# Regrouping the state, decay and factor work of blocks 0 and 1, and a last store in two row halves

## The chip, the cores and the metric

The kernel runs on one core of a Trainium2 chip. The metric is the device time of one execution in microseconds (us). A core has five engines that run side by side, each through its own instructions in order: TensorE (PE, with its weight loads listed as PEld), VectorE (DVE), ScalarE (ACT), GpSimd (POOL) and SyncE (SP, which here only issues transfers). An instruction that needs another engine's result waits on a semaphore, and everything behind it on its own engine waits with it. PE's results go to PSUM, which this kernel lays out as eight tiles of 128 x 512 float32, called banks here; what POOL takes of PSUM is copied to SBUF by ACT first.

## The reference

A chunked state-space layer (4 batches, 8 heads, 768 positions, head size 32, state size 16) is followed by a bilinear feed-forward layer over 3072 tokens of width 256 and inner width 1536.

```python
# per batch and head, chunk c of 32 positions
cum = np.cumsum(log_a[c]);  L = np.exp(cum[:, None] - cum[None, :]) * causal
y[c] = ((C @ B.T) * L) @ x  +  (C @ state) * np.exp(cum)[:, None]
state = np.exp(cum[-1]) * state + (B * np.exp(cum[-1] - cum)[:, None]).T @ x
# then, with heads and head sizes side by side as 256 columns
out = ((y @ w_a) * (y @ w_b)) @ w_out
```

The chunk length doesn't change the result, and the kernel takes chunks of 128.

## The kernel before

**Tiling.** The 768 positions are six blocks of 128. A block holds two "pairs"; pair p belongs to block p // 2. Block 0 (pairs 0 and 1) is treated batch by batch with its own code; from block 1 on (pairs 2 to 11) the work is laid out by batch in `planes`, turned into `BT` and `CT` by a VectorE transpose (`turn`). The running product of `a` within a block stands in `Pr`, its middle row's inverse in `rmid`, and the decay factors are made from both: `fB`, `fC` (lines 781, 790, 871) for block 0 and the state of block 1, `FC` and its inverse `FB` for the planes, `fCl` and `fBl` for the states of the later blocks.

**Factors.** `mid_rows` (286) multiplies `Pr` by `rmid` into `Ps` on POOL. `turned_rows` (296) is a VectorE transpose of `Ps` into `Pt`; `batch_factors` (301) copies `Pt` into `FC`, one copy for each of four batches, on ACT or on POOL; `batch_inverse` (308) is a VectorE reciprocal into `FB`; `late_factors` (311) and `late_inverse` (315) make `fCl` and `fBl` on VectorE. `scale_q` (341, called twice by `prep`) multiplies B or C by `FB` or `FC` into `planes` on POOL; `scale_bc` (324) does so for the states' B.

**Layer and states.** `scores` (398) is the small matmuls C·B into the four banks `SC`; `mask` (442) multiplies a bank by the causal table, on VectorE, or by an ACT copy and POOL; `pv1` (522) and `outputs` (532) multiply by x and copy the result out as `X2T` (block 0) or `XB`. `ds_mm` (495) makes a block's contribution to the state, and `gps` (852) spreads the blocks' decays over the state's rows; ACT copies it to `G` (861), from which POOL makes `Ge` (880), `spair` (576) and `gV` (586).

**Feed-forward.** A unit is a group of matmuls with `Wa` (`aps`), one with `Wb` (`bps`), an ACT copy of `aps` to SBUF (`evac_a`, 610, tile `asb`) and a VectorE product of `bps` and `asb` into `hk` or `hkb`. For block 0 a unit is (pair, k2) with four matmuls of 256 columns in each group (`unit_mm`, 593; `times`, 615); for later blocks it is `bunit(blk, k)` (659), with two of 512 columns. `out_mm`, `out_store` (634, 646) and `bout` (685) multiply by `Wo` and store.

**Order.** The schedule is manual: each engine runs its instructions in the order of the calls from line 774 on. Half of the PSUM banks are `SC`; the other four hold, one tile each, whatever `bank()` hands out, and the string `BANKS` (22) says which bank the n-th tile gets. A tile's first matmul waits until the tile before it in that bank has been read: an `aps` by its ACT copy, a `bps` by its VectorE product. The first tile (`fps`, factors and `gps`) keeps bank 0 until line 871 has read it; the next tile in that bank is the nineteenth, `aps` of unit (0, 4) (line 888).

**Transfers.** Loads of x as f16 and of the weights are issued by POOL (they change the type), all others by SP or ACT. `load_wo` (187) issues half of `Wo`. `bout(last, 3, 2)` (1036) ends the kernel: two halves of 128 columns, each with its own copy out of PSUM and its own store, the first by SP, the second by ACT (709).

Of the kernel before, what the change touches and what calls it, by code (L numbers as in the profile page):

```python
# [19 lines left out]
SS = 64.0  # L20

BANKS = (
    "012313213212312312031203123021032103120312013201320130231021302130231203120312013023102310"
    "2312013201320132012301230123012301230123012301320132013201320132013201320132013201320"
)


# [1 line left out]
def kernel(  # L29
# [13 lines left out]
    nc = tc.nc  # L43

    nb, H, S, D = x.shape
# [5 lines left out]
    NK = d_ff // 128  # L51
    NQ = NK // 2
    BH = nb * H
    NBP = nb // 2
# [74 lines left out]
    def bank(name):  # L129
        return psf.tile([128, 512], f32, name=name, tag=f"ff{next(banks)}")  # L130
# [56 lines left out]
    def load_wo(half):  # L187
        return nc.gpsimd.dma_start(
            Wo[:, 6 * half : 6 * half + 6].rearrange("p (g kk) e -> p g (kk e)", kk=3),
            moe_w_out.rearrange("(g p kk) e -> p g (kk e)", p=128, kk=3)[:, 2 * half : 2 * half + 2],  # L190
        )
# [94 lines left out]
    def mid_rows(lo, hi, eng):  # L286
        k = slice(lo + NBLK - NT, hi + NBLK - NT)
        eng.tensor_tensor(
            out=Ps[:, lo:hi], in0=Pr[:, k], in1=rmid[:, k].unsqueeze(2).broadcast_to((BH, hi - lo, Q)), op=ALU.mult
        )  # L290
# [5 lines left out]
    def turned_rows(lo, hi):  # L296
        nc.vector.transpose(
            Pt[:, lo:hi].rearrange("p k s c -> p (k s) c"), Ps[:, lo:hi].rearrange("p k (i s) -> p k s i", s=4)
        )
# [8 lines left out]
    def batch_inverse(lo, hi):  # L308
        nc.vector.reciprocal(FB[:, lo:hi], FC[:, lo:hi])

    def late_factors(lo, hi):
        for c0 in range(32 * lo, 32 * hi, 32):
            nc.vector.transpose(fCl[c0 : c0 + 32], Ps[:, NT - NL :, c0 : c0 + 32])
# [4 lines left out]
    def flat(f, lo, hi):  # L318
        return f[:, lo:hi].rearrange("p k r b h -> p (k r b h)")
# [175 lines left out]
    def ds_mm(p, DS):  # L495
        s, bp = st[p], p % NBP
        st["DS", p // NBP] = DS
        DS = DS.rearrange("p (g d) -> p g d", d=2 * D)
        for bt, g in itertools.product(range(2), range(4)) if p >= P2 else ():
            row = 32 * (2 * bp + bt)  # L500
            nc.tensor.matmul(  # L501
                DS[row : row + 32, g],
                s["bm"][:, bt, 2 * g : 2 * g + 2, :].rearrange("p h n -> p (h n)"),
                by_token(s["X16"])[:, bt, 2 * g : 2 * g + 2].rearrange("p h d -> p (h d)"),
                start=True,
                stop=True,
                skip_group_check=True,
                tile_position=(0, row),
            )
        for r, g, bt in itertools.product(range(2), range(4), range(2)) if p < P2 else ():  # L510
            k, row = slice(64 * bt, 64 * bt + 64), 32 * (2 * bp + bt)
            nc.tensor.matmul(
                DS[row : row + 32, g],
                s["bm"][k, r, 2 * g : 2 * g + 2, :].rearrange("p h n -> p (h n)"),
                s["X16"][k, 2 * g : 2 * g + 2, r, :],
                start=(r == 0 and g == 0),
                stop=(r == 1),
                skip_group_check=True,
                tile_position=(64 * bt, row),
            )  # L520

    def pv1():
        PY = [SC1[:, bt, 0:256] for bt in range(2)]
        for u in range(2):
            pv_u(1, u, PY, True)
        o_ = X2T[:, 1].rearrange("p t u q -> p t (u q)")
        i_ = SC1[:, :, 0:256]
        c0 = nc.scalar.activation(out=o_[:, 0], in_=i_[:, 0], func=AF.Copy, scale=YS / SS)
        c1 = nc.vector.tensor_scalar(o_[:, 1], i_[:, 1], YS / SS, None, ALU.mult)
        tc.declare_no_dep(c1.ins, c0.ins.name, reason="reads of two banks")  # L530
# [79 lines left out]
    def evac_a(a_ps, on_dve=False):  # L610
        asb = ffh.tile([128, 512], f32, name="asb", tag="asb")
        (nc.vector.tensor_copy if on_dve else nc.scalar.copy)(asb, a_ps)  # L612
        return asb
# [12 lines left out]
    def unit(p, k2, between=None, by_pool=False):  # L626
        a_ps = unit_mm(p, k2, Wa)
        if between:
            between()
        b_ps = unit_mm(p, k2, Wb)  # L630
        asb = evac_a(a_ps)
        return lambda: times(p, k2, b_ps, asb, by_pool)

    def out_mm(p, bt, o_ps, ks):
        hk = st[p]["hk"]
        for k in ks:
            nc.tensor.matmul(  # L637
                o_ps[:, 0:d_model],
                hk[:, k, bt * Q : (bt + 1) * Q],
                Wo[:, k, :],  # L640
                start=(k == 0),
                stop=(k == NK - 1),
                skip_group_check=True,
            )
# [36 lines left out]
    def bgo(blk, *ks):  # L681
        for k in ks:
            bunit(blk, k)()

    def bout(blk, c, parts=1):
        hk = st[("FF", blk)]["hk"]
        rows = out[c * S + blk * Q :][0:Q]
        w = d_model // parts
        for part in range(parts):
            o_ps = bank("ops")  # L690
            cs = slice(part * w, part * w + w)
            for k in range(NK):
                nc.tensor.matmul(  # L693
                    o_ps[:, 0:w],
                    hk[:, k, c * Q : (c + 1) * Q],
                    Wo[:, k, cs],
                    start=(k == 0),
                    stop=(k == NK - 1),
                    skip_group_check=True,
                )  # L700
            o_sb = outp.tile([128, d_model], f32, name="osb", tag="osb")
            if parts > 1 and part == 0:
                nc.vector.tensor_scalar(o_sb[:, 0:w], o_ps[:, 0:w], 1.0 / (YS * YS), None, ALU.mult)
            else:
                nc.scalar.activation(out=o_sb[:, 0:w], in_=o_ps[:, 0:w], func=AF.Copy, scale=1.0 / (YS * YS))  # L705
            if blk * NBP < P0:
                stores.append(lambda rows=rows, o_sb=o_sb: nc.sync.dma_start(rows, o_sb))
            else:
                (nc.sync, nc.scalar)[part].dma_start(rows[:, cs], o_sb[:, 0:w])

    def loads_b(*ps):
        for p in ps:
# [16 lines left out]
    def loads_x(p):  # L729
        if p < NP:  # L730
            load2(nc.gpsimd, p, 2)

    def go(*items):
        for p, k2 in items:
            unit(p, k2)()
# [111 lines left out]
    loads_b(4, 5)  # L847
    times(0, 0, bps[0], asb[0])
    times(0, 1, bps[1], asb[1], by_pool=True)
    pv1()  # L850
    ds_mm(1, SC[0][:, 0:256])
    gps = fps[:, 96 : 96 + H // 2 * NG]
    nc.tensor.matmul(
        gps,
# [3 lines left out]
        stop=True,  # L858
        skip_group_check=True,
    )  # L860
    nc.scalar.copy(G.rearrange("p g k -> p (g k)"), gps)
    times(0, 2, bps[2], asb[2])
    turned_rows(0, 1)
    load_wo(0)
    batch_factors(0, 1, *range(nb), eng=nc.gpsimd)
    mid_rows(1, NT, nc.gpsimd)
    go((1, 0))
    batch_inverse(0, 1)
    go((1, 1))
    ds_mm(0, SC[0][:, 0:256])  # L870
    nc.vector.reciprocal(flat(fB, 1, 2), fps[:, 2 * NBP * H : 4 * NBP * H])
    go((1, 2))
    scale_q(2, 1, nc.gpsimd)
    scale_q(3, 1, nc.gpsimd)
    scale_q(2, 0, nc.gpsimd)
    load_wo(1)
    scale_q(3, 0, nc.gpsimd)
    state_sums(0)
    late_factors(0, 3)
    nc.gpsimd.tensor_tensor(  # L880
        out=Ge.rearrange("p k (g e) -> p g k e", e=2),
        in0=G.unsqueeze(3).broadcast_to((128, H // 2, NG, 2)),
# [4 lines left out]
    late = ((0, 3), (0, 4), (1, 3))  # L887
    aps = [unit_mm(p, k2, Wa) for p, k2 in late]
    asb = [evac_a(a_ps) for a_ps in aps]
    for (p, k2), a_sb_ in zip(late, asb):  # L890
        times(p, k2, unit_mm(p, k2, Wb), a_sb_)
        if k2 == 4:
            turn(2)
    go((0, 5))
    h = unit(1, 4, lambda: scores(2))
    turn(3)
    mask(product(2, 3), by_pool=True)
    mask(product(2, 0))
# [2 lines left out]
    mask(product(2, 2), by_pool=True)  # L901
    load_q(nc.gpsimd, 2, ALL_Q[6:])
    mask(product(2, 1))
    turned_rows(1, 2)
    o = [bank("ops"), bank("ops")]
    out_mm(0, 0, o[0], range(6))
    out_mm(0, 1, o[1], range(6))
    batch_factors(1, 2, 0, 1)
    h5()
    scores(3)  # L910
    mask(product(3, 3), by_pool=True)
    batch_factors(1, 2, 2, 3)
# [5 lines left out]
    )  # L918
    for m in range(3):
        mask(product(3, m))  # L920
    batch_inverse(1, 2)
    turned_rows(2, NT)
    for bt in range(2):
        o.append(bank("ops"))
        out_mm(1, bt, o[-1], range(6))
    for f in x_in:
        f()
    for c in range(3):
        p, bt = divmod(c, NBP)
        out_mm(p, bt, o[c], range(6, NK))  # L930
        if c == 2:
            batch_factors(2, NT, *range(nb))
        out_store(p, bt, o[c])
    loads_q(3)
    prep(4)
    prep(5)
    loads_x(4)
    late_factors(3, 4)
    late_inverse(0, NL)
    outputs(1)  # L940
    state_sums(1)
    batch_inverse(2, NT)
    prep_b(4, 5)
    loads_b(6, 7)
    out_mm(1, 1, o[3], range(6, NK))
# [8 lines left out]
    for m in range(3):  # L954
        mask(product(4, m))
        if m == 0:
            loads_x(6)
            prep(6)
        if m == 1:
            turn(5)  # L960
        bgo(1, *range(4 + 3 * m, min(7 + 3 * m, NK)))
    scores(5)
    mask(product(5, 3), by_pool=True)
    prep(7)
# [102 lines left out]
```

## Time and profile before

| | |
|---|---|
| time, median of 3 runs (lowest, highest) | 123.44 us (123.11, 123.44) |
| the profiled execution's own time | 122.69 us |
| its span, first to last instruction | 120.8 us |
| granted TensorE clock over the span | 1.000 |
| DMA moved | 12.13 MB, mean 100 GB/s |

| stretch, us | PE | DVE | ACT | POOL busy, us |
|---|---|---|---|---|
| 10 to 15 | 4.83 | 4.55 | 3.62 | 3.23 |
| 15 to 20 | 5.00 | 4.06 | 3.48 | 3.41 |
| 20 to 25 | 5.00 | 4.92 | 2.99 | 4.91 |
| 25 to 30 | 4.96 | 4.93 | 4.02 | 4.92 |
| 40 to 45 | 4.97 | 5.00 | 2.73 | 3.83 |
| 110 to 121 | 7.55 | 1.84 | 2.70 | 0.00 |

The busy time of PE counts each matmul from its start to a modelled end, and a matmul's end overlaps the next one's start, so PE is busy by this count even in a pause of some tenths of a microsecond. Pauses are better read from the starts of successive groups: a group of four matmuls of 256 columns, or of two of 512, takes 0.43 to 0.44 us from its start to the next group's.

### The profile page before, as it was taken

The page shows a single profiled execution, that of the slowest core. Times are in us where ns is not written, and L with a number is a line of the kernel's source. Part 1 is how long each engine was busy: PE and PEld are TensorE (multiplying, and loading weights), DVE is VectorE, ACT ScalarE, POOL GpSimd, SP SyncE. Part 2 cuts the span into 40 slices and gives each one's busy share as a digit, 9 for nine tenths or more (in the row PEclk, how much of TensorE's full clock was granted, in tenths as well). Part 3 has the DMA queues.
Part 4 walks back from the last instruction along what each step waited for, and adds up shares of the span by engine and source line. Part 5 has one row for each costly group of instructions (what it writes and reads, how often), then busy time and mean ns, then how long its engine had stood idle before and what let it go on. Part 6 is the DMA issues. An engine that isn't in the chain of part 4 may idle for free.

```text
span 120.8 us, 3551 instructions
## 1 busy us (share of the span) xinstructions
PE 115.9 (96%) x1385; PEld 73.9 (61%) x1386; DVE 90.2 (75%) x166; ACT 67.9 (56%) x136; POOL 58.8 (49%) x92
## 2 busy tenths in 40 slices
PE   7989999999999999999999999999999999999990
PEld 2436789888644488544485464775465684645880
DVE  5998988999798994599966999686899426758000
ACT  0446756769776646567666646635735637475230
POOL 7994986999699969387803994200000000000000
PEclk9999999999999999999999999999999999999999
DMA  3999999894789994959992929012001111010132
GB/s 63 135 183 192 207 230 197 134 200 113 99 94 161 115 139 101 110 68 121 218 241 89 85 9 121 5 46 87 5 6 40 43 49 44 0 43 0 43 108 71
DMA packets 59297, 12.13 MB, mean 100 GB/s; under 512 B 54480, under 2 KB 59216, under 8 KB 59280
## 3 DMA queue, kind: packets, MB, share of 16 engines
q0 software_dynamic: 20320, 3.80, 38.9%
q1 hardware_dynamic: 36432, 7.74, 34.8%
q10 hardware_dynamic: 2528, 0.36, 1.8%
q8 instruction: 11, 0.18, 0.7%
q14 instruction: 6, 0.05, 0.1%
HBM read 12.42 MB, written 3.15 MB: 129 GB/s over the span
## 4 chain that ended last, share of the span: by engine, by line
PE 92%; DVE 4%; issue 0%; ACT 0%
PE ops L693 22%; PE aps L667 22%; PE bps L667 21%; PE ops L637 5%; PE aps L598 4%; PE SC L404 4%; PE bps L598 3%; DVE t L449 3%; PE SC L238 3%; PE SC L473 2%; PE SC L536 1%; PE tc L238 1%; PE py L458 1%; PE SC L485 1%; DVE bt L385 1%
## 5 line engine op out<-in xcount | busy, mean ns | idle before, releaser
L612 ACT COPY asb<-aps 128x512 f32<-128x512 f32 x72 | 42.0, 587 | 17.2 <-PE aps L667 13.4
L679 DVE TENSOR_TENSOR hkb<-bps,asb 128x512 f16<-128x512 f32 x60 | 40.2, 687 | 12.7 <-ACT asb L612 11.1
L667 PE MATMUL aps<-XB,Wa 128*128 128x512 f16 x120 | 35.7, 379 | 0.0
L667 PE MATMUL bps<-XB,Wb 128*128 128x512 f16 x120 | 35.7, 379 | 0.0
L693 PE MATMUL ops<-Wo,hkb 128*128 128x256 f16 (+1 forms) x252 | 28.1, 268 | 0.0
L693 PEld LDWEIGHTS <-hkb 128*128 128x128 f16 x252 | 23.0, 98 | 3.8
L667 PEld LDWEIGHTS <-Wb 128*128 128x128 f16 x120 | 12.4, 103 | 13.6
L667 PEld LDWEIGHTS <-Wa 128*128 128x128 f16 x120 | 12.1, 103 | 11.7 <-issue 0.5
L449 DVE TENSOR_TENSOR t<-SC,causal_q 128x512 f16<-128x512 f32 x27 | 17.3, 681 | 2.4 <-PE SC L404 2.4
L705 ACT ACTIVATE osb<-ops 128x256 f32<-128x256 f32 (+1 forms) x20 | 7.6, 379 | 18.4 <-PE ops L693 18.4
L447 POOL TENSOR_TENSOR t<-tmp,causal_q 128x512 f16<-128x512 f32 x5 | 5.8, 1161 | 10.0 <-ACT tmp L446 10.0
L177 POOL DMA_DIRECT2D xn<-in_x_dram x8 | 9.5, 1192 | 0.0
L346 POOL TENSOR_TENSOR planes<-cq,FC 128x256 f16<-128x256 f32 x10 | 7.6, 775 | 2.2 <-DMA cq<-in_C_dram 2.1
L622 DVE TENSOR_TENSOR hk<-bps,asb 128x512 f16<-128x512 f32 x11 | 7.2, 672 | 0.9 <-ACT asb L612 0.8
L346 POOL TENSOR_TENSOR planes<-bq,FB 128x256 f16<-128x256 f32 x10 | 7.7, 772 | 0.4 <-DMA bq<-in_B_dram 0.4
L449 DVE TENSOR_TENSOR t<-SC,causal 128x512 f16<-128x512 f32 x11 | 7.0, 675 | 0.4 <-PE SC L404 0.3
L598 PE MATMUL aps<-X2T,Wa 128*128 128x256 f16 x48 | 6.8, 274 | 0.0
L446 ACT COPY tmp<-SC 128x512 f32<-128x512 f32 x10 | 5.9, 589 | 1.5 <-PE SC L404 1.1
L598 PE MATMUL bps<-X2T,Wb 128*128 128x256 f16 x48 | 6.6, 273 | 0.0
L558 ACT ACTIVATE XB<-SC 128x512 f16<-128x512 f32 (+1 forms) x9 | 4.6, 547 | 3.5 <-PE SC L501 2.4
L447 POOL TENSOR_TENSOR t<-tmp,causal 128x512 f16<-128x512 f32 x5 | 5.8, 1161 | 0.0
L637 PE MATMUL ops<-Wo,hk 128*128 128x256 f16 x48 | 5.8, 273 | 0.0
(101 smaller groups left out, 109.2 us busy)
## 6 DMA issues: line engine op xcount, KB each, us to landing
out_dram<-osb SPq DMA_DIRECT2D x23, 128.0 KB, 1.8
cq<-in_C_dram SPq DMA_DIRECT2D x20, 64.0 KB, 3.9
bq<-in_B_dram SPq DMA_DIRECT2D x18, 64.0 KB, 3.8
bn<-in_B_dram SPq DMA_DIRECT2D x8, 128.0 KB, 4.1
xn<-in_x_dram POOLq DMA_DIRECT2D x8, 128.0 KB, 5.9
Wa<-in_moe_w_a_dram POOLq DMA_DIRECT2D x2, 384.0 KB, 7.3
Wb<-in_moe_w_b_dram POOLq DMA_DIRECT2D x2, 384.0 KB, 7.9
Wo<-in_moe_w_out_dram POOLq DMA_DIRECT2D x2, 384.0 KB, 6.5
```

What stands on the lines that cost most here:

```text
L177: eng.dma_start(by_token(pair_in[p][which]).rearrange("p t h n -> p (t h) n"), src.rearrange("t h q n -> q (t h) n"))
L346: eng.tensor_tensor(out=plane[:, c0 : c0 + 4 * step].rearrange("p (j c) s -> p j s c", c=step)[:, :, :, 0:N], in0=by_batch[blk][which][:, ...
L447: nc.gpsimd.tensor_tensor(out=o_, in0=tmp, in1=c_, op=ALU.mult)
L449: nc.vector.tensor_tensor(out=o_, in0=i_, in1=c_, op=ALU.mult)
L598: nc.tensor.matmul(ps[:, kk * 2 * Q : (kk + 1) * 2 * Q], W[k // 6][:, f, k % 6 // 3 * 384 : (k % 6 // 3 + 1) * 384].rearrange("p (c kk) -> ...
L612: (nc.vector.tensor_copy if on_dve else nc.scalar.copy)(asb, a_ps)
L622: eng.tensor_tensor(out=s["hk"][:, 2 * k2 : 2 * k2 + 2, :].rearrange("p k q -> p (k q)"), in0=b_ps, in1=asb, op=ALU.mult)
L637: nc.tensor.matmul(o_ps[:, 0:d_model], hk[:, k, bt * Q : (bt + 1) * Q], Wo[:, k, :], start=(k == 0), stop=(k == NK - 1), skip_group_check= ...
L667: nc.tensor.matmul(t_, W[k // 6][:, f, k % 6 // 3 * 384 : (k % 6 // 3 + 1) * 384].rearrange("p (c kk) -> p kk c", kk=3)[:, k % 3], XB[:, b ...
L679: return lambda: nc.vector.tensor_tensor(out=s["hk"][:, k], in0=ps[1], in1=asb, op=ALU.mult)
L693: nc.tensor.matmul(o_ps[:, 0:w], hk[:, k, c * Q : (c + 1) * Q], Wo[:, k, cs], start=(k == 0), stop=(k == NK - 1), skip_group_check=True,)
L705: nc.scalar.activation(out=o_sb[:, 0:w], in_=o_ps[:, 0:w], func=AF.Copy, scale=1.0 / (YS * YS))
```

## The change

Nothing that is computed changes, and no load. What moves or is regrouped:

- `gps` is made before `pv1`; `ds_mm(0)` follows `ds_mm(1)` at once, and the copy to `G` is VectorE's in place of ACT's; the reciprocal of line 871 follows it, ahead of the product of unit (0, 2).
- `load_wo(1)` is issued four POOL operations earlier.
- `turned_rows` for blocks 2 to 5 is one call in place of two, in the place of `late_factors(0, 3)`, which moves behind the masks of pair 3; `batch_factors(2, NT)` moves ahead to the units at 890; `batch_inverse(1, NT)` is one call in place of two.
- `scores(2)` stands behind both groups of unit (1, 4), not between them.
- `out_mm(1, 0)` stands ahead of `scores(3)`, not behind it.
- `outputs(1)` and `state_sums(1)` stand ahead of `late_factors(3, 4)` and `late_inverse`.
- `turn(5)` stands behind unit 4 of block 1, not behind the mask that precedes unit 7.
- The second half of the last store is issued as rows 0 to 63 by ACT and rows 64 to 127 by SP.
- `BANKS` has another order.

```diff
 BANKS = (
-    "012313213212312312031203123021032103120312013201320130231021302130231203120312013023102310"
-    "2312013201320132012301230123012301230123012301320132013201320132013201320132013201320"
+    "012313213212301230123012302103120312301230132013210320132012301230132103210321023013201320"
+    "1321023102310231021302130213021302130213021302310231023102310231023102310231023102310"
 )
...
+            elif part == 0:
+                nc.sync.dma_start(rows[:, cs], o_sb[:, 0:w])
             else:
-                (nc.sync, nc.scalar)[part].dma_start(rows[:, cs], o_sb[:, 0:w])
+                for eng, h in ((nc.scalar, slice(0, 64)), (nc.sync, slice(64, 128))):
+                    eng.dma_start(rows[h, cs], o_sb[h, 0:w])
...
-    pv1()
-    ds_mm(1, SC[0][:, 0:256])
     gps = fps[:, 96 : 96 + H // 2 * NG]
     nc.tensor.matmul(
         gps,
...
-    nc.scalar.copy(G.rearrange("p g k -> p (g k)"), gps)
+    pv1()
+    ds_mm(1, SC[0][:, 0:256])
+    ds_mm(0, SC[0][:, 0:256])
+    nc.vector.tensor_copy(G.rearrange("p g k -> p (g k)"), gps)
+    nc.vector.reciprocal(flat(fB, 1, 2), fps[:, 2 * NBP * H : 4 * NBP * H])
     times(0, 2, bps[2], asb[2])
     turned_rows(0, 1)
     load_wo(0)
     batch_factors(0, 1, *range(nb), eng=nc.gpsimd)
     mid_rows(1, NT, nc.gpsimd)
+    load_wo(1)
     go((1, 0))
     batch_inverse(0, 1)
     go((1, 1))
-    ds_mm(0, SC[0][:, 0:256])
-    nc.vector.reciprocal(flat(fB, 1, 2), fps[:, 2 * NBP * H : 4 * NBP * H])
     go((1, 2))
     scale_q(2, 1, nc.gpsimd)
     scale_q(3, 1, nc.gpsimd)
     scale_q(2, 0, nc.gpsimd)
-    load_wo(1)
     scale_q(3, 0, nc.gpsimd)
     state_sums(0)
-    late_factors(0, 3)
+    turned_rows(1, NT)
...
     asb = [evac_a(a_ps) for a_ps in aps]
+    batch_factors(2, NT, *range(nb))
     for (p, k2), a_sb_ in zip(late, asb):
         times(p, k2, unit_mm(p, k2, Wb), a_sb_)
         if k2 == 4:
             turn(2)
     go((0, 5))
-    h = unit(1, 4, lambda: scores(2))
+    h = unit(1, 4)
+    scores(2)
     turn(3)
...
     mask(product(2, 1))
-    turned_rows(1, 2)
     o = [bank("ops"), bank("ops")]
     out_mm(0, 0, o[0], range(6))
     out_mm(0, 1, o[1], range(6))
     batch_factors(1, 2, 0, 1)
     h5()
+    o.append(bank("ops"))
+    out_mm(1, 0, o[2], range(6))
     scores(3)
...
-    batch_inverse(1, 2)
-    turned_rows(2, NT)
-    for bt in range(2):
-        o.append(bank("ops"))
-        out_mm(1, bt, o[-1], range(6))
+    batch_inverse(1, NT)
+    late_factors(0, 3)
+    o.append(bank("ops"))
+    out_mm(1, 1, o[3], range(6))
...
-        if c == 2:
-            batch_factors(2, NT, *range(nb))
         out_store(p, bt, o[c])
...
     loads_x(4)
+    outputs(1)
+    state_sums(1)
     late_factors(3, 4)
     late_inverse(0, NL)
-    outputs(1)
-    state_sums(1)
-    batch_inverse(2, NT)
...
-        if m == 1:
+        k0 = 4 + 3 * m
+        bgo(1, k0)
+        if m == 0:
             turn(5)
-        bgo(1, *range(4 + 3 * m, min(7 + 3 * m, NK)))
+        bgo(1, *range(k0 + 1, min(k0 + 3, NK)))
```

## The prediction

> **What bounds the kernel now.** I read the page's engine shares and chain first, then the waits of PE, then the timeline.
>
> ```profile
> PE 115.9 (96%) x1385; PEld 73.9 (61%) x1386; DVE 90.2 (75%) x166; ACT 67.9 (56%) x136; POOL 58.8 (49%) x92
> ...
> PE 92%; DVE 4%; issue 0%; ACT 0%
> ```
>
> PE is the chain: 92% of it, and from 14.85 us to 117.6 us nothing else. The count of matmuls doesn't change, so only pauses between groups, PE time spent on changing between kinds of matmul, and the tail can change. The starts of groups in the timeline (start, length, engine, line) show them:
>
> ```profile
> 12.16 1.55 PE L598 MATMUL bps<-X2T,Wb 128*128 128x256 f16 x12
> ...
> 13.64 0.45 PEld L458 LDWEIGHTS <-xn 64*32 64x32 f16 x32 [0.20 <-issue]
> ...
> 13.86 0.42 PE L458 MATMUL SC<-t,xn 64*32 64x128 f16 x32
> ...
> 14.37 0.42 DVE L529 TENSOR_SCALAR X2T<-SC 128x256 f16<-128x256 f32 x1
> 14.43 0.29 PEld L853 LDWEIGHTS fps<-hsx,indm 32*128 32x128 f32 x2
> ...
> 14.85 0.62 PE L598 MATMUL aps<-X2T,Wa 128*128 128x256 f16 x4
> ...
> 16.20 0.60 PE L598 MATMUL bps<-X2T,Wb 128*128 128x256 f16 x4
> ...
> 16.73 0.41 PE L512 MATMUL SC<-xn,bm 64*32 64x64 f16 x16
> ```
>
> Four places lose time. (a) `pv1` has its weights at 13.64 but starts at 13.86, when VectorE's mask has ended (13.80): 0.22 us. (b) `ds_mm(0)` breaks the units: from bps at 16.20 to the second bps after it at 17.52 are 1.32 us where two periods of 0.4375 are due, so it costs 0.445, of which 0.09 is the change of tile size ahead of it (16.20 to 16.73 is 0.53, not 0.44). (c) and (d) are here:
>
> ```profile
> 23.89 1.47 PE L637 MATMUL ops<-Wo,hk 128*128 128x256 f16 x12
> ...
> 24.67 0.68 DVE L449 TENSOR_TENSOR t<-SC,causal 128x512 f16<-128x512 f32 x1
> ...
> 25.40 0.65 PE L404 MATMUL SC<-turned 32*64 32x128 f16 x32
> ...
> 39.91 1.85 DVE L679 TENSOR_TENSOR hkb<-bps,asb 128x512 f16<-128x512 f32 x3
> 39.98 0.59 PE L667 MATMUL bps<-XB,Wb 128*128 128x512 f16 x2
> ...
> 40.61 0.59 PE L667 MATMUL aps<-XB,Wa 128*128 128x512 f16 x2
> ```
>
> (c) Twelve matmuls at 0.109 and the size change of 0.09 should lead to `scores(3)` at 25.29; it starts at 25.40, behind VectorE's last mask (24.67 + 0.68): 0.11 us. (d) 39.98 to 40.61 is 0.63 where 0.43 is the rule: 0.20 us, because the bank is that of bps 7, whose product is the first of VectorE's three from 39.91.
>
> **The change, part by part.**
>
> *gps, pv1 and both ds_mm.* `gps` now starts in pause (a), at 13.64; its input is ready since 12.62 (POOL, 12.41 + 0.21). The rows bound its price: 0.29 (its two weight loads) to 0.42 (14.43 to 14.85, but that end was set by VectorE's copy, 14.37 + 0.42). I take 0.29, as the next small loads need wait for nothing else: `pv1` at 13.93, 0.07 later than now (0.20 at the other end). Then `pv1` 0.25, `ds_mm(1)` 0.33 and `ds_mm(0)` 0.34 end at 14.85. VectorE's copy of `X2T` starts 0.51 behind `pv1`, at 14.44, ends at 14.86, and aps (1, 0) starts 0.06 behind it, as now, at 14.92. So `ds_mm(0)` lies wholly under that copy: **-0.445 + 0.07**.
>
> *VectorE behind it.* Its instructions overlap by 0.08 when nothing holds them. New ahead of product (0, 2) are the copy to `G` and the reciprocal. No row has the copy on VectorE; copies from PSUM of 128 and 256 columns are 0.29 and 0.42, so 20 columns give some 0.18 (bounds 0.15, its shortest reciprocal, and 0.29). G 14.78 to 14.96, reciprocal (0.34) to 15.22, product (0.68) to 15.82, `turned_rows` (0.39) to 16.13. POOL's four copies to `FC` take 0.96 (15.86 to 16.82 now), so 16.21 to 17.17. The product of (1, 0), which waits for ACT's copy, is done at 16.94; next in VectorE's queue is `batch_inverse`, which stands until 17.20 (now 16.85, when VectorE had just come free) and ends at 17.56. Queued behind it is the product of (1, 1), 17.48 to 18.14. **Who waits: PE.** By the new string aps (0, 4) takes the bank of bps (1, 1), while before it took that of `fps`. PE, in steps of 0.4375 from 14.92, would be there at 18.00 and must wait until 18.20: **+0.20** (0 if `FC` is copied faster or G is short, 0.35 with the long G and late POOL). All other banks of the new order are free in time: bps (1, 1) wants bank 1 at 16.25 (read until 15.82), bps (1, 2) bank 3 at 17.12 (17.00), bps (0, 3) bank 3 at 19.07 (18.80).
>
> *turned_rows(1, NT) and the four ACT copies.* POOL's `mid_rows` (1.04) follows `FC`: ready at 18.29. VectorE reaches the transpose at 18.66. Its price: 128 columns 0.374, 384 columns 0.776, so 512 give 0.98 by the slope, 1.58 as four times 0.394; I take 0.98, since 384 already lie on that slope: done at 19.64, about as `late_factors` now (19.87). ACT's four copies (0.25 to 0.27 each, 1.09 with gaps) then run from 19.92, behind the copy of aps (1, 3), to 21.01. Queued behind is the copy of aps (0, 5), wanted at 21.06; it ends at 21.65, and bps (1, 4) takes that bank at 21.70: **0**, with no cover to spare.
>
> *load_wo(1).* Its 0.76 of issue lies at 18.29 to 19.05 in POOL's idle time (now idle until 19.32, when the C of block 1 has landed): 0; and `scale_q(3, 0)` comes 0.75 earlier. Its data go ahead of x and B of block 1 in the queues: x of pairs 2 and 3 landed at 24.05, ACT's casts want it at 27.4, so 1.9 (384 KB at the 200 GB/s of these slices) can be hidden.
>
> *scores(2) behind unit (1, 4).* Planes still end at 21.31, `turn(2)` at 21.92; PE comes there at 22.14, so 0.
>
> *out_mm(1, 0) ahead of scores(3).* Its 0.66 covers pause (c): VectorE's mask ends at 25.35, PE comes at 25.67 with 0.09 of size change to go: **-0.11**.
>
> *Inverse, late factors, outputs(1).* VectorE ends pair 3's masks at 28.37, `batch_inverse` of 128 columns (0.95, as `fBl`) at 29.24, three transposes of 0.30 at 30.09; its copy to `XB` is wanted at 30.15. Cover 0.06, then 0.13 more before PE needs `XB`: 0.
>
> *turn(5).* Behind product 4 (ends 37.17) it lasts to 37.66, product 5 is 0.23 late, product 6 on time, the mask ends at 39.50, so product 7 ends at 40.07 and not at 40.55; aps 10 wants its bank at 40.41: **-0.20**.
>
> *The last store.* The tail:
>
> ```profile
> 117.59 0.28 ACT L705 ACTIVATE osb<-ops 128x128 f32<-128x128 f32 x1 [0.96 <-PE ops L693]
> 117.90 0.38 ACTq L709 DMA_DIRECT2D out_dram<-osb  x1
> ```
>
> SP ends its own issue at 117.65 and then only waits, so both halves start at 117.90. The issue costs 0.65 for 512 pieces and 0.45 for 256, 0.0008 a piece: 64 rows in place of 128 save 0.05. Landing takes 1.6 for 64 KB and 1.8 to 1.9 for 128 KB, so half the bytes would save 0.15 if each half had engines to itself. Bounds +0.10 (SP's half late) and -0.20; I take **-0.06**. By the Trainium skill (DMA: Bandwidth & Descriptors, Rules for kernel authors) two transfers to disjoint partition halves aren't worth making, as both are spread over the same 16 engines; only issue time is saved. By that rule this term would be -0.05, and the further 0.14 in rival 1 is not to be had; no row here shows two such halves.
>
> **Sum**: -0.445 + 0.07 + 0.20 - 0.11 - 0.20 - 0.06 = **-0.55**. Against the profiled execution (span 120.85, time 122.69; 1.84 lies around the span) that gives 120.3 and 122.14. The median of the runs shown is 0.75 above that execution; on it the forecast is **122.9**. About 0.3% (0.37 us) is what a measurement of this kernel can tell from no change.
>
> **Rivals.**
>
> 1. *No wait at aps (0, 4), store at its best.* For it: the wait of 0.20 hangs on 0.26 that VectorE stands before `batch_inverse`, a chain of four short instructions. Against: each link has a row. -0.55 - 0.20 - 0.14 = -0.89: **122.55**. Chance 0.18.
>
> 2. *The bank takes the gain.* VectorE's delay is at its upper end: G 0.29 and later POOL copies make the wait 0.35; `gps` costs 0.42 (+0.13); the store gives nothing (+0.06). -0.55 + 0.15 + 0.13 + 0.06 = -0.21: **123.2**, the same. For it: bounds of rows; against: all three together. Chance 0.20.
>
> 3. *ACT stands on `Pt` (slower).* Place: the four ACT copies ahead of the copy of aps (0, 5). From `Pt` at 19.64 on, every 0.1 costs PE 0.1 at bps (1, 4). With the transpose at 1.58, `Pt` comes at 20.24, ACT ends at 21.63, aps (0, 5) is copied at 22.24 and bps (1, 4) starts at 22.30, +0.60; from +0.55 on it decides. With the long `gps` as well (+0.13) and the store at +0.10: -0.55 + 0.60 + 0.13 + 0.16 = +0.34: **123.8**. For it: no cover at all there; against: the slope of the two transposes. Chance 0.15.
>
> **How the numbers follow.** Forecast 0.47 (122.65 to 123.1), rivals 0.18, 0.20, 0.15. Predicted 122.9. The range takes in rivals 1 and 2 and the nearer part of 3: 122.3 to 123.6. Faster by over 0.3%: forecast and rival 1, 0.65; within: rival 2 and 0.02 of rival 3, 0.22; slower: 0.13.
>
> **What would show it.** `gps` ahead of `pv1`, `pv1` near 13.93 and aps (1, 0) near 14.92, with no small matmuls up to `scores(2)`; a step of some 0.64 in place of 0.44 before aps (0, 4); no wait before `scores(3)`; even steps of 0.43 through block 1's units; ACT's `FC` copies ended by 21.05 and bps (1, 4) without a step; two half issues at the same time and an end some 2.9 us behind them. It is wrong if a step of over 0.3 appears at aps (0, 4), bps (1, 4) or the first matmul on `XB`.

## The result, and the profile after

The changed kernel is slower: 123.37 us median of 21 runs against 122.86 us of 21 runs of the kernel before, a ratio of 1.0037 with a 95% interval of 1.0025 to 1.0048. One of the changed kernel's 21, at 137.4 us with a granted clock of 0.857, is left out of the ratio. Its profiled execution took 123.15 us with a span of 121.45 us; before these were 122.69 and 120.85.

The page's engine shares and its chain, after:

```profile
PE 115.1 (95%) x1385; PEld 73.4 (60%) x1386; DVE 90.2 (74%) x165; ACT 67.5 (56%) x135; POOL 58.6 (48%) x92
...
q8 instruction: 11, 0.18, 0.6%
...
PE 88%; DMA 4%; SPq 2%; DVE 2%; issue 1%; ACT 0%; DVEq 0%
```

PE's busy time falls by 0.8 us though it runs the same 1385 matmuls: somewhere it now stands, long enough to show in this count. Where, the waits of PE show (line and what it waited for, us in total, times, longest):

```profile
PE SC L238 <- PEq L1055: 0.8, 1, 0.8
PE SC L512 <- issue: 0.7, 1, 0.7
```

The first was there before. The second is new: line 512 is `ds_mm`, its 0.7 us are counted from the modelled end of the matmul before, and "issue" means that no wait which the profile shows explains it. In the timeline after:

```profile
13.75 0.39 PE L854 MATMUL fps<-hsx,indm 32*128 32x20 f32 x2
...
14.07 0.42 PE L458 MATMUL SC<-t,xn 64*32 64x128 f16 x32
...
14.32 0.45 PE L512 MATMUL SC<-xn,bm 64*32 64x64 f16 x25
...
14.59 0.42 DVE L529 TENSOR_SCALAR X2T<-SC 128x256 f16<-128x256 f32 x1
14.94 0.17 DVE L865 COPY G<-fps 128x20 f32<-128x20 f32 x1
...
15.49 0.27 PE L512 MATMUL SC<-xn,bm 64*32 64x64 f16 x7 [0.71 <-issue]
...
15.70 0.62 PE L598 MATMUL aps<-X2T,Wa 128*128 128x256 f16 x4
```

`gps` stands ahead of `pv1`, as planned, and VectorE's copy of `X2T` ends at 15.02, so aps (1, 0) could start at 15.08. But 25 of the 32 matmuls of the two `ds_mm` run, the last of them starts at 14.59 and the next matmul only at 15.49, and aps (1, 0) starts at 15.70: 1.62 us behind `pv1` and not 1.00.

The pauses that the change was forecast to remove are gone. Ahead of `scores(3)`, and in block 1's units:

```profile
24.28 2.13 PE L637 MATMUL ops<-Wo,hk 128*128 128x256 f16 x18
26.34 0.65 PE L404 MATMUL SC<-turned 32*64 32x128 f16 x32
...
40.26 0.59 PE L667 MATMUL bps<-XB,Wb 128*128 128x512 f16 x2
40.69 0.59 PE L667 MATMUL aps<-XB,Wa 128*128 128x512 f16 x2
```

Eighteen matmuls at 0.109 and the size change of 0.09 make the 2.06 from 24.28 to 26.34, and 40.26 to 40.69 is the even step of 0.43.

The end, after:

```profile
117.67 0.28 ACT L705 ACTIVATE osb<-ops 128x128 f32<-128x128 f32 x1 [0.96 <-PE ops L693]
117.97 0.55 SPq L712 DMA_DIRECT2D out_dram<-osb  x1
117.98 0.57 ACTq L712 DMA_DIRECT2D out_dram<-osb  x1
```

Two issues of half the rows last 0.55 and 0.57 where one of all rows lasted 0.38. From the end of the last copy to the end of the span it is 3.50 us; before it was 2.98.

So in the two profiled executions the last copy ends 0.08 later (117.95 against 117.87) and the tail is 0.52 longer: the difference of the spans is 0.60, nearly all of it behind the last matmul. The 0.62 of the new pause has eaten the middle's gain.

### The profile page after: what moved, and what is told of

The parts are those of the page before. It is cut to its first block, busy times and chain, and to the rows that moved or that the text cites. A ratio compares the mean times of both kernels' runs of the same rounds, so it can differ in the third digit from the quotient of the medians.

```text
span 121.5 us, 3551 instructions
## 1 busy us (share of the span) xinstructions
PE 115.1 (95%) x1385; PEld 73.4 (60%) x1386; DVE 90.2 (74%) x165; ACT 67.5 (56%) x135; POOL 58.6 (48%) x92
## 4 chain that ended last, share of the span: by engine, by line
PE 88%; DMA 4%; SPq 2%; DVE 2%; issue 1%; ACT 0%; DVEq 0%
PE ops L693 22%; PE aps L667 22%; PE bps L667 21%; PE aps L598 5%; PE ops L637 4%; PE bps L598 4%; DMA bn<-in_B_dram 4%; PE SC L404 3%; PE SC L473 2%; SPq L153 2%; PE SC L536 1%; PE SC L485 1%; DVE t L449 1%; PE SC L512 0%; DVE cm L333 0%
```

## Experiments

The ratios are to the kernel before, run on the same chip.

**The split store alone.** The kernel before with this edit only:

```diff
+            elif part == 0:
+                nc.sync.dma_start(rows[:, cs], o_sb[:, 0:w])
             else:
-                (nc.sync, nc.scalar)[part].dma_start(rows[:, cs], o_sb[:, 0:w])
+                for eng, h in ((nc.scalar, slice(0, 64)), (nc.sync, slice(64, 128))):
+                    eng.dma_start(rows[h, cs], o_sb[h, 0:w])
```

> The kernel before, with the last store in two row halves and nothing else changed. Theory A (the two halves are what makes the end late): their issues last about 0.55 us each in place of 0.38, the second half lands some 2.1 us after its issue in place of 1.6, the end comes 0.5 us later, ratio to before about 1.004. Rival (the late end belongs to that one profiled execution): issues of 0.38 or less, ratio 0.999 to 1.001.

```profile
119.11 0.54 SPq L712 DMA_DIRECT2D out_dram<-osb  x1
119.11 0.56 ACTq L712 DMA_DIRECT2D out_dram<-osb  x1
```

Measured: 123.56 us against 122.81, ratio 1.0070 (1.0045 to 1.0094), tail 3.52 us. The store is a loss by itself. The ratio is somewhat above the 1.004 that a tail longer by 0.5 accounts for; what the rest is isn't shown (in its profiled execution `pv1` also waited for a late load of x, 0.74 us, a load that the edit doesn't touch).

**The change without the split store.** The changed kernel with line 709 as before.

> The changed kernel with the last store in one piece, as before. Theory A: 0.5 us less than the changed kernel, so about as before, ratio to before 0.998 to 1.001, and the pause of 0.9 us inside ds_mm(0) is still there. Rival (the store is no part of the loss): ratio 1.003 to 1.004.

Measured: 122.65 us against 122.81, ratio 0.9985 (0.9966 to 1.0004), tail 2.98 us. The pause is still there:

```profile
14.19 0.42 PE L458 MATMUL SC<-t,xn 64*32 64x128 f16 x32
14.44 0.46 PE L512 MATMUL SC<-xn,bm 64*32 64x64 f16 x25
15.49 0.27 PE L512 MATMUL SC<-xn,bm 64*32 64x64 f16 x7 [0.59 <-issue]
```

`ds_mm` starts 0.12 later than in the changed kernel's profile, and PE goes on at the same 15.49. Whatever it waits for comes at a time of its own, 15.49 in both profiles.

**More PE instructions ahead of the pause.** As the last, with ten warm-up matmuls of 512 columns cut in two, for instance:

```diff
-    warmup(SC[3], 512, 512, 128)
+    warmup(SC[3], *4 * [256], 128)
...
-    warmup(tcp, 512)
+    warmup(tcp, 256, 256)
```

> As the one before it, with ten warm-up matmuls of 512 columns made as twenty of 256: the same PE time, 20 PE instructions more ahead of the pause. Theory F (PE has run out of delivered instructions, since a block of them is asked for at a fixed count and takes over 2 us): the block is asked for about 1 us earlier, the pause in ds_mm(0) falls from 0.9 to under 0.2 us, aps (1, 0) starts near 15.0 in place of 15.7; with a wait of up to 0.2 us then at aps (0, 4), the ratio to before is about 0.996. Rival (the two ds_mm side by side hold each other up): the pause stays at 0.9 us and the ratio at 0.998 to 1.001.

Measured: 122.33 us against 122.81, ratio 0.9956 (0.9929 to 0.9983). `pv1` to aps (1, 0) is 1.00 us, with the two `ds_mm` side by side as before:

```profile
14.47 0.42 PE L458 MATMUL SC<-t,xn 64*32 64x128 f16 x32
14.72 0.67 PE L512 MATMUL SC<-xn,bm 64*32 64x64 f16 x32
15.47 0.51 PE L598 MATMUL aps<-X2T,Wa 128*128 128x256 f16 x3
```

So it isn't the neighbourhood of the two groups. (The profiled execution, at 123.54 us, is the longest of its twelve: B of block 1 landed at 21.54 and not near 20, and PE waited 0.9 us in two places for `turn`. Its aps (1, 0), expected near 15.0, is at 15.47 because `pv1` too starts 0.4 us later than in the changed kernel's profile, 14.47 and 14.07.)

**Half as many more.** Five warm-ups cut in two.

> The changed kernel with the last store in one piece and five warm-up matmuls of 512 columns made as ten of 256 (10 PE instructions more; the run with ten pairs had 20). Theory F: the block of instructions is asked for some 0.5 us earlier, so the pause in ds_mm(0) is between that of none more (0.79 and 0.90) and of 20 more (none): 0.2 to 0.5 us, and five pairs of matmuls earlier in the group, since the block ends at a fixed count. Rival (the two ds_mm side by side): 0.8 to 0.9 us, at the same matmul.

```profile
14.10 0.42 PE L458 MATMUL SC<-t,xn 64*32 64x128 f16 x32
14.35 0.72 PE L512 MATMUL SC<-xn,bm 64*32 64x64 f16 x32
15.10 0.62 PE L598 MATMUL aps<-X2T,Wa 128*128 128x256 f16 x4
```

Measured in one execution: a pause of 0.15 us, below the range expected, at exactly the place expected (too short for the timeline to break the row of `ds_mm`, which lasts 0.72 us here and 0.67 with 20 rows more). This table is read from the single PE rows of the traces (weight loads and matmuls, counted from the first, with two rows of the program's start). The packet is the first of 16384 bytes in the instruction queue q8 behind the start. A pause is taken from one row's start to the next's. Times are in us:

```
kernel                     packet, from-to   rows by then   pause at row       resumes   pv1 to aps (1, 0)
before                     13.12 - 14.08     324            none               -         1.00
changed                    13.15 - 14.12     322            448: 0.90          15.49     1.62
changed, store as before   13.16 - 14.12     322            448: 0.79          15.49     1.51
  and 10 rows more         12.45 - 13.41     318            448: 0.15          14.72     1.00
  the same, run again      12.24 - 13.21     311            none               -         1.00
  and 20 rows more         12.59 - 13.54     326            449: 0.06          14.98     1.00
  and ds_mm(0) back        13.15 - 14.10     316            none               -         1.00
```

With 10 and 20 rows more ahead of it, another matmul of `ds_mm` stands at the pause, five and ten pairs further up; the row number stays. And wherever PE pauses, it goes on 1.31 to 1.45 us behind the end of the packet. In the second execution with 10 rows more PE comes to row 448 at 14.93, 1.72 behind the packet's end, and doesn't pause. The reading that fits all of this: a block of PE instructions ends there, and the next one has not come. It is inferred, since the profile doesn't say which engine a packet is for. The packet starts 311 to 326 rows in, some 125 rows ahead of the pause, and in the units, at two rows in 0.109 us, 125 rows would last several microseconds; with the burst of `gps`, `pv1` and two `ds_mm` among them they take 1.43 us in the changed kernel (13.15 to 14.59). Before, row 448 lay in the units, at about 15.7, and the block was there.

By the Trainium skill (Runtime: NRT & Kernel Launch, Instruction fetch mechanics) instructions come in blocks of 16 KiB, 256 of them, fetched while the block before runs, and crossing a block's end is mostly hidden. The trace agrees with the size of the blocks (11 packets, 0.18 MB in q8); in PE rows the packets of the changed kernel start 186 to 366 apart, 240 on average. But this one crossing was not hidden: it costs 0.5 to 0.6 us on the path.

**ds_mm(0) back between the units.** The changed kernel, the store as before, and:

```diff
     ds_mm(1, SC[0][:, 0:256])
-    ds_mm(0, SC[0][:, 0:256])
...
     go((1, 1))
+    ds_mm(0, SC[0][:, 0:256])
```

> The changed kernel with the last store in one piece and ds_mm(0) back behind unit (1, 1). Theory F: the burst of short instructions ahead of aps (1, 0) is 64 instructions shorter, so PE reaches the end of the block only in the units, when the next one is there: no pause; aps (1, 0) near 15.0 us, 0.44 us for ds_mm(0) later; ratio to before 0.996 to 0.999. Rival (the pause belongs to the waits around pv1 and gps, not to the count): a pause of over 0.5 us ahead of aps (1, 0) stays.

Measured: 122.67 us against 122.78, ratio 0.9988 (0.9967 to 1.0010), no pause, `pv1` to aps (1, 0) 1.00 us. The waits around `gps` and `pv1` are not its cause. By the ratio alone this can't be told from the version with the pause: 0.445 us for `ds_mm(0)` between the units are about what the pause costs.

**The kernel before with the finer warm-ups**, a control.

> The kernel before with the same ten warm-up matmuls made as twenty. Theory F: before has no pause of that kind, so nothing is to be gained: ratio 0.998 to 1.002. Rival (finer warm-ups are faster by themselves, whatever the order behind them): 0.995 to 0.997.

Measured: 122.79 us against 122.78, ratio 1.0002 (0.9980 to 1.0023). The warm-ups gain nothing by themselves.

**The version with ten rows more, timed.**

> The kernel of the run with five pairs of warm-ups again, timed: the changed kernel with the last store in one piece and 10 PE instructions more. Theory F with the store as the only loss of the change besides the pause: pv1 to aps (1, 0) 1.00 us as in one look of it, ratio to before 0.994 to 0.997. Rival (the look was a lucky execution, and early loads make up for part of it): 0.998 to 1.000.

Measured: 122.47 us against 123.16, ratio 0.9952 (0.9929 to 0.9975), `pv1` to aps (1, 0) 1.00 us. By these ratios this version is faster than both kernels.

**What makes the split store slow.** Other forms of the last piece in the kernel before, one execution each, so that their issues and landings are read and not their total times. First, 64 rows alone; the kernel leaves out the other 64:

```diff
+                nc.scalar.dma_start(rows[0:64, cs], o_sb[0:64, 0:w])
```

> The kernel before, storing of its last 128 x 128 piece only rows 0 to 63, by ACT; rows 64 to 127 of that piece are left out. Theory R (a store of 64 rows is itself the slower form): issue about 0.55 us, first data some 1.2 us after it, as in the changed kernel. Theory C (two issues at one time hold each other up): issue 0.38 us or less, first data 0.9 us or less after it, end no later than before.

```profile
118.06 0.55 ACTq L711 DMA_DIRECT2D out_dram<-osb  x1
```

With nothing beside it the issue still lasts 0.55, its first data move 1.21 us behind the issue and the last landing comes 1.86 behind it. Theory C falls as the main cause. Then both halves by columns (`rows[:, cs][:, h]`, `o_sb[:, h]`):

> The kernel before, with its last 128 x 128 piece stored as two column halves of 128 rows and 256 bytes a row, by ACT and SP at one time. Theory R+C (the form of 64 rows costs 0.17 at the issue and some 0.3 to the first data; two stores issued at one time are carried out one behind the other, 0.27 apart): issues of 0.38, the first half's data start 0.9 us behind the issue, the second's some 0.3 behind them, and the last landing comes 0.1 to 0.3 us later than the 1.60 of one piece. Rival (only the number of transfers counts): issues of 0.55 and a last landing 2.1 us behind the issue, as with row halves.

```profile
117.81 0.33 SPq L712 DMA_DIRECT2D out_dram<-osb  x1
...
117.81 0.38 ACTq L712 DMA_DIRECT2D out_dram<-osb  x1
```

Two at one time, 128 rows each: issues as ever, first data at 0.83 and 0.94, last landing 1.65 behind the issue. Being two costs 0.05, less than the 0.1 to 0.3 expected; the second half's data don't wait for the first's here. Next, whether any part of the rows is slow: 96 and 32 rows alone, the kernel leaving out the others:

> The kernel before, storing of its last 128 x 128 piece only rows 0 to 95, by ACT; rows 96 to 127 of that piece are left out. Theory R1 (any store of fewer than 128 rows is the slower form): issue 0.5 us or more, first data 1.1 us or more behind it. Theory R2 (only the half is slow): issue 0.38, first data 0.9.

> The kernel before, storing of its last 128 x 128 piece only rows 0 to 31, by ACT; rows 32 to 127 of that piece are left out. Theory R1: issue 0.5 us or more, first data 1.1 us or more behind it, though only a quarter is moved. Theory R2: issue 0.38 or less, first data 0.9 or less.

```profile
118.33 0.36 ACTq L711 DMA_DIRECT2D out_dram<-osb  x1
```

That is the line of 96 rows; that of 32 has the same 0.36. First data 0.86 behind the issue in both, landings at 1.55 and 1.42. So it isn't true of any part of the rows: of 128, 96, 64 and 32 only 64 is slow. Last, the change's own split at another row:

> The kernel before, with its last 128 x 128 piece stored in two row parts as in the change, but of 96 rows (ACT) and 32 rows (SP). Theory R2 (the loss is that of the 64-row form, doubled since the second half's data come behind the first's): issues of 0.36 to 0.38, first data 0.86 to 1.0 us behind them, last landing 1.5 to 1.7 us behind the issue, so about the 1.60 of one piece. Rival (two row parts issued at one time are slow, whatever their size): issues of 0.5 or more and a last landing of 1.9 us or more.

```profile
118.21 0.36 SPq L712 DMA_DIRECT2D out_dram<-osb  x1
...
118.22 0.38 ACTq L712 DMA_DIRECT2D out_dram<-osb  x1
```

Last landing 1.64 behind the issue, tail 3.02: the loss of 0.5 is gone, and nothing is gained over one piece (1.60, 2.98). The parts of the tail side by side, read from the traces, us behind the (last) issue:

```
last piece                issue         first data      last landing   copy's end to span's end
one piece (before)        0.38          0.89            1.60           2.98
64 + 64 rows (changed)    0.55, 0.57    1.21, 1.48      2.12           3.50
64 rows alone             0.55          1.21            1.86           3.24
64 + 64 columns           0.33, 0.38    0.83, 0.94      1.65           3.03
96 + 32 rows              0.36, 0.38    0.86, 0.91      1.64           3.02
96 rows alone             0.36          0.86            1.55           2.93
32 rows alone             0.36          0.86            1.42           2.80
```

The change's 0.52 is 0.26 that the 64-row form costs alone, and 0.26 because the second half's data start, at 1.48, when the first's have all been sent (the last of them at 1.48 too). Why 64 rows are slow stays open: no run here looks below the issue.

## Why the prediction was wrong

The direction was wrong, by two terms. No rival has a pause of this kind, and none has a store dearer than +0.10. The forecast of 122.9 stood on 123.44, the median of three runs of the kernel before, which is 122.86 over 21 runs; that 123.37 lies in the stated range of 122.3 to 123.6 is owed to this, and is luck. Point by point:

- **The last store, taken as -0.06, measured +0.52.** I took the issue's price from a slope over loads of 512 and 256 pieces. No row had a store of 64 rows, and the upper bound, +0.10, assumed that nothing but a late start of SP could cost. The slope doesn't hold for these stores at all: 32 and 96 rows take the same 0.36 to issue, and 64 rows 0.55. The rule of the Trainium skill that I weighed there (DMA: Bandwidth & Descriptors, Rules for kernel authors: halves aren't worth it) has the right verdict by the forms of 96 + 32 rows and of columns, which gain nothing; the form used is worse than that.
- **"ds_mm(0) lies wholly under that copy", -0.445 + 0.07, failed by more: it measured +0.29.** As a mechanism it is right. With the block of instructions there, `pv1` to aps (1, 0) measures 1.00 us, as summed (13.93 to 14.92). In the changed kernel 0.62 is lost to the pause, which the prediction put at nothing, and the step nets a loss (-0.445 + 0.11 + 0.62, with `pv1` 0.11 later). I priced instructions by their durations and never asked whether PE would have them.
- `gps`: 0.29 taken, 0.32 measured (13.75 to 14.07), its bounds held. The copy to `G` on VectorE: 0.18 taken, 0.17 measured.
- The wait at aps (0, 4): 0.20 forecast, none in the changed kernel, since the pause makes PE late there, and about 0.05 in the versions with 10 and 20 rows more (steps of 0.48 to 0.50 in place of 0.44).
- Pauses (c) and (d): -0.11 and -0.20, both right, shown by the steps above.
- `turned_rows` over 512 columns: 0.98 taken, 1.12 measured. ACT's four copies then end at 21.60, the copy of aps (0, 5) starts at 21.65 and PE has no step at bps (1, 4): the slower rival, ACT standing on `Pt`, didn't come about. The pause doesn't explain this: in the versions with 10 and 20 rows more, where PE comes earlier, that step is at most 0.46 too.
- `load_wo(1)`, `scores(2)`, the late factors and `outputs(1)` at nothing: no step in PE at any of them.

The sum over the terms as measured: -0.445 + 0.11 (`pv1` behind the mask: 0.17 in place of 0.05) + 0.62 - 0.11 - 0.20 + 0.52 = +0.50, with the first loads 0.10 late in that execution: 0.60, the difference of the spans. The version with ten rows more has neither 0.62 nor 0.52 but the wait of 0.05: -0.445 + 0.11 + 0.05 - 0.11 - 0.20 = -0.60, and it measures -0.59 (0.0048 of 123.16; by the interval -0.31 to -0.87, so the agreement to 0.01 is chance).

## What to carry to other kernels

When many short matmuls are put side by side, count instructions as well as time. Here the packet for PE's next instructions started about 125 rows ahead of where they were needed, and it took 2.3 to 2.4 us from the packet's start until PE went on; a stretch that ran through these rows in 1.4 us stood, with nothing else to wait for. Ten or twenty cheap instructions more ahead of it made the pause short or none, and a pause that stays at one row number while the code moves under it is how to tell. Look at the price of the exact form of a transfer before splitting it: here no split of the last store gained, and one cost half a microsecond.

## What the runs showed that I had not expected

- A store of 64 rows of 512 bytes takes longer to issue (0.55 us) and to start moving (1.21) than one of 128 (0.38 and 0.89), 96 or 32 rows (0.36 and 0.86).
- PE stood for up to 0.90 us, from one matmul's start to the next's, with no wait that the profile shows; by the row number and the packets its instructions had not come. The gap shows as "issue" in the waits and in the chain.
- From the end of the packet until PE goes on it is 1.31 to 1.45 us, more than the packet's own 0.95 to 0.96.
